# Keys and values pooled by VectorE in one reducing step each, and a free engine for the rests of the first weights

## The chip, the cores and the metric

The kernel runs on one core of a Trainium2 chip. The metric is the device time of one execution in microseconds (us), as the median of several runs. TensorE is written PE (PEld for its weight loads), VectorE DVE, ScalarE ACT, GpSimd POOL, and SyncE, which only issues transfers here, SP.

## The reference, cut to what matters

Eight batches of attention with pooled keys and values, then two wide feed-forward layers over 4608 tokens of 512 features. The part that the change touches is the pooling: eight neighbouring positions of a sequence of 576 are averaged into one, which leaves 72.

```python
# q, k, v: (8 batches, 8 heads, 576, 64) fp32
k_p = k.reshape(B, H, 72, 8, D).mean(axis=3)
v_p = v.reshape(B, H, 72, 8, D).mean(axis=3)
scores = scale * q @ k_p.transpose(0, 1, 3, 2)
attn_out = softmax(scores) @ v_p
# layer 1, x (8, 576, 512) from attn_out: u = x + (x^T U V)^T ; y = u + relu(u @ w_ch1) @ w_ch2
# layer 2: layer norm of y, then relu(yn @ w2_ch1) @ w2_ch2, added to y
```

## The kernel before

Every piece of work is declared as an operation with a price for each engine that may do it, with what it reads and writes, and with a priority. A planner in the file (`Order.schedule`) then lays all operations out in one go: it keeps a clock for each engine, gives an operation that two engines may do to the one that its prices favour, allocates buffers from rings, and treats VectorE and GpSimd as shut out of one another while both work on SBUF. The order that it arrives at is written into the program of each engine, and each engine follows its own list strictly. A changed price or a changed list of engines can therefore move any later operation.

The work goes through two heads at a time, called a pair: 32 pairs (`P`), four to a batch. For each pair SP loads `k` (128 rows: two heads by 64 features; 576 positions along a row), `q` and `v` (72 rows: one for each pooled position; for each head 8 times 64 numbers along the row). There is one buffer each for `k` and `v`, and two for `q`. `att_prep` pools the keys into `kp` and scales them into `kbd`; `att_prep_v` pools the values into `vs` (or `v1` for the first two batches, P below `TM` = 8); then come scores, softmax and the product with `vs`. From P = 8 on, `vs` holds a high part, rounded to the fp32r format, and the rest, so that two fast matmuls stand for one exact one; `split` makes such a pair of tensors.

In parallel the weights of layer 1 arrive as 64-bit floats. `load_w` decodes eight blocks of them in two halves each (lines 594 to 621, mostly VectorE), and splits each half into `wh` and its rest `wl` (line 556). The other weights are decoded later and parked in DRAM (`ahead`). The first eight blocks are used by `a_l1` (line 1291) and `a_l2` (line 1319) on tokens that are already through attention, while attention goes on for the later batches; this stretch ends near 600 us. After it three passes with the remaining weights run to the end (lines 1520 and 1608), with no pooling in them.

Before, the pooling of keys can be done by VectorE in one `tensor_reduce` (line 796) or by GpSimd in three halving additions (lines 799 and 800). The values are pooled by three halving additions, 512, 256 and 128 wide over both heads, each on either engine (line 827). The rest `wl` is for GpSimd alone.

Of the kernel before, what the change touches and what calls it, by code (L numbers as in the profile page):

```python
# [14 lines left out]
ALU = mybir.AluOpType  # L15
AX = mybir.AxisListType
# [3 lines left out]
B, H, S, D = 8, 8, 576, 64  # L20
DM = 512
NT = B * S
POOL = 8
SP = S // POOL
# [26 lines left out]
class Ring:  # L51


    def __init__(self, pool, shape, dtype, n, name, fifo=True):
        self.pool, self.shape, self.dtype, self.n, self.name, self.fifo = pool, shape, dtype, n, name, fifo
        self.tiles, self.free, self.made, self.turn = None, [(0.0, i) for i in range(n)], 0, 0
        pool.rings.append(self)
# [34 lines left out]
PE, ACT, DVE, GP, SY = "pe", "act", "dve", "pool", "sync"  # L92
# [273 lines left out]
def c_dve(n):  # L366
    return 68 + 1.042 * n


def c_fast(n):  # L370
    return 68 + 0.521 * n


def c_act(n, ps=False):
    return (51 if ps else 93) + 0.8333 * n


def c_pool(n):
    return 147 + 2.11 * n
# [28 lines left out]
def scaled(nc, e, dst, src, by):  # L408
    if e is nc.scalar:
        e.mul(dst, src, by)  # L410
    else:
        e.tensor_scalar(dst, src, by, None, op0=ALU.mult)
# [9 lines left out]
class Kern:  # L422
    def __init__(self, nc, tc, aps):
        self.nc, self.tc = nc, tc
        (self.qT, self.kT, self.v, self.U, self.V, self.wA, self.g, self.wC, self.out) = aps
        self.w_raw = [self.wA, self.wC]
        self.o = Order(nc, tc)
        att = Pool("att")
        stg = Pool("stg")
        slots = Pool("slots", side="right")  # L430
        w = Pool("wres", side="right")
        b1 = Pool("b1", after=[att])
        b2 = Pool("b2", side="right", after=[w])
        ps = Pool("ps", space=PSUM)
        self.pools = [stg, att, slots, w, ps, b1, b2]
        R = self.R = {}

        def ring(pool, name, shape, dt=F32, n=1, fifo=True):
            R[name] = Ring(pool, shape, dt, n, name, fifo)

        ring(stg, "wraw", [128, 512], I64)
        ring(stg, "wx", [128, 512])
        ring(stg, "wt", [128, 512])
        ring(att, "araw", [128, 512], I64)
        ring(att, "ax", [128, 512])
        ring(att, "at", [128, 512])
        ring(att, "kbd", [128, 2, SP], n=2)
        ring(att, "q", [128, S], n=2)
        ring(att, "k", [128, S])
        ring(att, "v", [SP, 2, POOL * D])  # L450
        ring(att, "kp", [128, SP], n=2)
        ring(att, "vs", [SP, 4, D], F32R, 3)
        ring(att, "vz", [SP, 3 * D], n=2)
        ring(att, "ef", [SP, 2, S])
        ring(att, "sc", [128, 5, 2 * SP], n=2)
        ring(att, "mx", [128, 10], n=2)
        ring(att, "sm", [128, 10], n=2)
        ring(att, "eh", [SP, 2, S], F32R)
        ring(att, "el", [SP, 2, S], F32R)
        ring(att, "avt", [128, SH], n=2)  # L460
        ring(att, "xT", [128, S], n=5)
        ring(att, "xh", [128, DM], F32R, 2)
        ring(att, "xl", [128, DM], F32R, 2)
        ring(att, "gr", [128, DM], F32R)
        ring(att, "gs", [128, DM], F32R)
        ring(att, "ust", [128, 5, 128], F32R)
        ring(att, "us", [128, 5, 128])
        ring(att, "vd", [128, S // 4], F32R, 2)
        ring(att, "v1", [SP, 2, D + 1], n=2)
        ring(att, "x4", [128, DM])  # L470
        ring(att, "ut", [128, 4 * 64])
        ring(att, "vstk", [128, S], F32R)
        ring(slots, "op", [128, SLOT], F32R, 16)
        ring(slots, "hid", [128, SLOT], F32R, 8)
        for f in range(NA):
            for a in "hl":
                ring(w, f"w{a}{f}", [128, 1024], F32R)
        ring(w, "xg", [128, NCC, TG])
        ring(w, "ys", [128, TG], n=2)
        for j in range(NSL):  # L480
            pool = b1 if j < NSL - 1 else b2
            for a in "hl":
                ring(pool, f"w1{a}{j}", [128, 7, 256], F32R)
                ring(pool, f"w2{a}{j}", [128, 2, 512], F32R)
        ring(b1, "xraw", [128, NCC, TG])
        ring(b1, "t3", [128, 2, TH])
        ring(b1, "t2", [128, 2, TH])
        ring(b2, "s12", [128, TG], n=2)
        ring(b2, "s5", [128, TH], n=2)
        ring(b2, "res", [128, NCC, TG], n=2)  # L490
        ring(b2, "yt", [128, NCC, TG])
        for a in ("lnh", "lnl"):
            ring(b2, a, [128, TG], F32R)
        for a in ("lns", "lnq"):
            ring(b2, a, [128, TG])
        for a in ("lnv", "lnd"):
            ring(b2, a, [128, TG // 128])
        ring(ps, "pa", [128, 512], n=2)
        ring(ps, "pbc", [128, 512], n=2, fifo=False)
        ring(ps, "py", [128, 512], n=4)  # L500
# [244 lines left out]
    def load_w(self, f, z, way):  # L745

        if z == 0:
            self.wres[f] = self.buf(f"wh{f}"), self.buf(f"wl{f}")
        wh, wl = self.wres[f]
        x = self.decoded(0, f, z, way)  # L750
        c = slice(z * 512, z * 512 + 512)
        self.split(View(wh, z, lambda t: t[:, c]), View(wl, z, lambda t: t[:, c]), View(x, None, lambda t: t), 512, hi_on=(ACT,), lo_on=(GP,))

    def ahead(self, layer, f, z):

# [32 lines left out]
    def att_prep(self, P):  # L788
        nc, o = self.nc, self.o
        q, k, v = self.raw[P]  # L790
        kp, kbd = self.buf("kp"), self.buf("kbd")
        kv = lambda: k.t.rearrange("p (n s) -> p n s", s=POOL)

        def pool(e):
            if e is nc.vector:
                e.tensor_reduce(kp.t, kv(), axis=AX.X, op=ALU.add)
                return
            for n in (4, 2):
                e.tensor_add(kv()[:, :, :n], kv()[:, :, :n], kv()[:, :, n : 2 * n])
            e.tensor_add(kp.t, kv()[:, :, 0], kv()[:, :, 1])  # L800

        o.op({DVE: c_dve(S), GP: c_pool(4 * SP) + c_pool(2 * SP) + c_pool(SP)}, pool, w=[k, kp])
        for h in range(2):
            r = slice(64 * h, 64 * h + 64)
            o.op(
                {ACT: c_act(SP), DVE: c_fast(SP)},
                lambda e, r=r, h=h: scaled(nc, e, kbd.t[r, h], kp.t[r], -1.0 / (POOL * 8)),
                r=[kp],
                w=[(kbd, h)],
            )  # L810
        self.qk[P] = (q, kbd)

    def att_prep_v(self, P):
        o = self.o
        v = self.raw[P][2]
        vs = self.vs[P] = self.buf("v1" if P < TM else "vz" if P < LEAN_T else "vs")
        n = POOL * D
        while n > D:
            n //= 2
            to, w = (lambda n=n: v.t[:, :, :n]), [v]  # L820
            if P < LEAN_T and n == D:
                to, w = (lambda: vs.t.rearrange("p (a d) -> p a d", d=D)[:, 0:3:2]), [v, vs]
                if P < TM:
                    to = lambda: vs.t[:, :, :D]
            o.op(
                {GP: c_pool(2 * n), DVE: c_dve(2 * n)},
                lambda e, n=n, to=to: e.tensor_add(to(), v.t[:, :, :n], v.t[:, :, n : 2 * n]),
                w=w,
            )
        if P < LEAN_T:  # L830
            return
        self.split(
            View(vs, 0, lambda t: t[:, 0:4:3]),
            View(vs, 1, lambda t: t[:, 1:3]),
            View(v, None, lambda t: t[:, :, :D]),
            2 * D,
        )

# [993 lines left out]
TM = 2 * NP  # L1832
E_BIAS = -40000.0
LEAN_T = 8
# [52 lines left out]
```

## Time and profile before

| | us |
|---|---|
| runs, median of 3 | 1762.2 (1757.46 to 1763.09) |
| the profiled execution, its own time | 1756.11 |
| its span in the trace | 1754.3 |
| PE busy in it | 1729.4 |
| DVE busy | 959.6 |
| POOL busy | 753.9 |

The span runs from the first to the last instruction. Busy time of PE counts a matmul from its start to its modelled end, so neighbouring matmuls overlap in it. A row that groups instructions gives the busy time of all of them, the mean of one in ns, and after the bar the idle time of the engine just before them, with what ended it.

### The profile page before, as it was taken

To read this page: it belongs to the slowest core of one execution; us is meant where nothing else is said; L and a number is where in the kernel's file an instruction comes from. 1 tells how busy PE (TensorE), PEld (TensorE's weight loads), DVE (VectorE), ACT (ScalarE), POOL (GpSimd) and SP (SyncE) were. 2 spreads that over 40 slices of the span, in tenths; PEclk is the share of its full clock that TensorE was granted. 3 is DMA by queue.
4 is the path that set the end of the run, shared out by engine and by line. 5 is a ranking of instruction groups with operands and counts; after the bars stand their busy time and mean duration, and the time that the engine had idled before them with its cause. 6 is when DMAs were issued, how large, how long until landed. Compare 5 with 4: busy or idle time off the path is not lost.

```text
span 1754.3 us, 27128 instructions
## 1 busy us (share of the span) xinstructions
PE 1729.4 (99%) x10302; PEld 1525.7 (87%) x10302; DVE 959.6 (55%) x1839; ACT 714.5 (41%) x1812; POOL 753.9 (43%) x655
## 2 busy tenths in 40 slices
PE   6999999999999999999999999999999999999998
PEld 6888888888888899999999889999999999999997
DVE  7998887888655344444445756553225633333333
ACT  5765655655522233333333443333333332223221
POOL 3442312311100166666667643333335455555554
PEclk9999999999999999999999999999999999999999
DMA  6665554555143334444443453431112422333322
GB/s 201 217 201 170 184 182 147 179 174 162 55 165 108 130 111 121 121 121 121 120 121 115 126 163 125 134 121 67 49 49 85 144 103 103 110 119 103 103 79 78
DMA packets 96691, 222.99 MB, mean 127 GB/s; under 512 B 15408, under 2 KB 15792, under 8 KB 90800
## 3 DMA queue, kind: packets, MB, share of 16 engines
q1 hardware_dynamic: 96416, 221.26, 39.9%
q8 instruction: 80, 1.31, 0.3%
q14 instruction: 51, 0.42, 0.1%
q10 hardware_dynamic: 144, 0.00, 0.0%
HBM read 151.85 MB, written 69.37 MB: 126 GB/s over the span
## 4 chain that ended last, share of the span: by engine, by line
PE 91%; DVE 2%; DMA 1%; POOL 0%; issue 0%; ACT 0%; DVEq 0%; POOLq 0%; ACTq 0%
PE py L1608 33%; PE pa L1520 17%; PE pbc L1520 13%; PE pbc L1319 11%; PE pa L1291 11%; PE py L398 2%; PE py L847 2%; PE py L978 1%; PE py L979 1%; PE py L1016 0%; PE py L1015 0%; DVE w1l L556 0%; PE py L1185 0%; PE pbc L1743 0%; DMA wraw<-w_d 0%
## 5 line engine op out<-in xcount | busy, mean ns | idle before, releaser
L1608 PE MATMUL py<-hid,w2h 128*128 128x512 f32 x1728 | 541.2, 394 | 0.2 <-DVE hid L1548 0.2
L1608 PE MATMUL py<-hid,w2l 128*128 128x512 f32 x864 | 338.7, 392 | 0.0
L1520 PE MATMUL pa<-op,w1h 128*128 128x256 f32 x1728 | 326.2, 281 | 1.4 <-DVE s L405 1.0
L1520 PEld LDWEIGHTS pa<-op,w1h 128*128 128x128 f32 x1728 | 293.8, 188 | 37.9 <-DVE s L405 1.5
L556 POOL TENSOR_TENSOR op<-xraw,op 128x512 fp32r<-128x512 f32 x130 | 171.9, 1324 | 276.9 <-ACT op L403 272.0
L1578 DVE TENSOR_TENSOR pbc<-s,pbc 128x512 f32<-128x512 f32 x108 | 75.2, 696 | 382.2 <-PE pbc L1520 382.2
L1608 PEld LDWEIGHTS py<-hid,w2h 128*128 128x128 f32 x1728 | 273.7, 189 | 11.1 <-DVE hid L1548 0.5
L1520 PEld LDWEIGHTS pbc<-op,w1h 128*128 128x128 f32 x1296 | 220.8, 188 | 28.1
L1520 PE MATMUL pbc<-op,w1h 128*128 128x256 f32 x1296 | 244.3, 281 | 0.0
L1520 PE MATMUL pa<-op,w1l 128*128 128x256 f32 x864 | 242.7, 281 | 0.0
L1608 PEld LDWEIGHTS py<-hid,w2l 128*128 128x128 f32 x864 | 162.5, 188 | 36.7
L1319 PE MATMUL pbc<-op,wh 128*128 128x512 f32 x576 | 182.1, 397 | 0.0
L1520 PE MATMUL pbc<-op,w1l 128*128 128x256 f32 x648 | 181.8, 281 | 0.0
L1291 PE MATMUL pa<-hid,wh 128*128 128x512 f32 x576 | 180.5, 394 | 0.0
L1520 PEld LDWEIGHTS pa<-op,w1l 128*128 128x128 f32 x864 | 163.0, 189 | 0.0
L1548 DVE SCALAR_TENSOR_TENSOR hid<-pa,hid 128x512 fp32r<-128x512 f32 x108 | 74.5, 690 | 125.1 <-ACT hid L1542 124.8
L1542 ACT ACTIVATE hid<-pa 128x512 fp32r<-128x512 f32 x108 | 64.6, 598 | 190.8 <-PE pa L1520 180.9
L1542 ACT ACTIVATE hid<-pbc 128x512 fp32r<-128x512 f32 x108 | 64.6, 598 | 180.4 <-DVE pbc L1578 179.5
L1474 POOL TENSOR_TENSOR t<-xraw 128x512 f32<-128x512 f32 x52 | 67.4, 1296 | 141.3 <-DMA xraw<-n_d 89.4
L1291 PEld LDWEIGHTS pa<-hid,wh 128*128 128x128 f32 x576 | 105.8, 188 | 21.3 <-DVE op L1298 0.2
L1520 PEld LDWEIGHTS pbc<-op,w1l 128*128 128x128 f32 x648 | 121.9, 188 | 0.0
L1319 PEld LDWEIGHTS pbc<-op,wh 128*128 128x128 f32 x576 | 103.8, 188 | 19.4
(210 smaller groups left out, 2864.2 us busy)
## 6 DMA issues: line engine op xcount, KB each, us to landing
xraw<-n_d SPq DMA_DIRECT2D x18, 1024.0 KB
wraw<-wC SPq DMA_DIRECT2D x32, 512.0 KB
wraw<-wA SPq DMA_DIRECT2D x24, 512.0 KB
w_d<-wx SPq DMA_DIRECT2D x48, 256.0 KB
wraw<-w_d SPq DMA_DIRECT2D x48, 256.0 KB
k<-kT SPq DMA_DIRECT2D x32, 288.0 KB
q<-qT SPq DMA_DIRECT2D x32, 288.0 KB
v<-v SPq DMA_DIRECT2D x32, 288.0 KB
```

The source lines that it names most:

```text
L398: e.matmul(out, src, ident, start=first, stop=True, is_transpose=True, skip_group_check=True)
L556: lambda e: e.tensor_sub(lo(), src(), hi().bitcast(F32)),
L847: lambda e: e.matmul(ps.t[:, i : i + 2 * SP], q.t[:, QT[t] : QT[t] + 128], kbd.t.rearrange("p h n -> p (h n)"), start=True, stop=True, ski ...
L978: e.matmul(ps.t[:, :SH], w, eh.t[:, h, c], start=True, stop=False)
L1291: e.matmul(ps.t, w.t[:, c], u.t, start=(i == 0), stop=(i == 3 * NCC - 1))
L1319: e.matmul(ps.t, w.t[:, c], x.t, start=(f == 0 and j == 0), stop=(f == NA - 1 and j == 2))
L1474: o.op(on, lambda e: e.tensor_sub(dst(), a(), c()), r=r, w=w)
L1520: e.matmul(bank.t[:, sl], w.t[:, self.WCOL[k], c], u.t[:, t], start=(first and i == 0), stop=(last and i == 5), skip_group_check=True,)
L1542: lambda e: e.activation(h.t[:, :TG], bank.t, AF.Relu),
L1548: lambda e: e.scalar_tensor_tensor(l.t[:, :TG], bank.t, 0.0, h.t[:, :TG].bitcast(F32), op0=ALU.max, op1=ALU.subtract),
L1578: o.op({DVE: c_dve(TG)}, lambda e: e.tensor_add(c.t, s.t, c.t), r=[s], w=[c])
L1608: e.matmul(y.t, w.t[:, i, c], x.t[:, :TG], start=(first and q == 0), stop=(last and q == 2))
```

## The change

Keys: only VectorE may pool them, in the one `tensor_reduce` that it had already. Values: only VectorE, in one `tensor_reduce` that reads `v` through the view `"p h (s d) -> p h d s"`, so that the eight numbers that are summed lie 64 numbers apart along the row; it reads 1024 numbers a row and writes 128. For P below `TM` it writes into `v1`; from then on into a new small buffer `vp` (one, 72 rows by 2 by 64), from which the split makes `vs`. Rests of the first weights: VectorE or GpSimd.

```diff
+        ring(att, "vp", [SP, 2, D])
...
-        self.split(View(wh, z, ...), View(wl, z, ...), View(x, None, ...), 512, hi_on=(ACT,), lo_on=(GP,))
+        self.split(View(wh, z, ...), View(wl, z, ...), View(x, None, ...), 512, hi_on=(ACT,))
...
-        def pool(e):
-            if e is nc.vector:
-                e.tensor_reduce(kp.t, kv(), axis=AX.X, op=ALU.add)
-                return
-            for n in (4, 2):
-                e.tensor_add(kv()[:, :, :n], kv()[:, :, :n], kv()[:, :, n : 2 * n])
-            e.tensor_add(kp.t, kv()[:, :, 0], kv()[:, :, 1])
-
-        o.op({DVE: c_dve(S), GP: c_pool(4 * SP) + c_pool(2 * SP) + c_pool(SP)}, pool, w=[k, kp])
+        o.op({DVE: c_dve(S)}, lambda e: e.tensor_reduce(kp.t, kv(), axis=AX.X, op=ALU.add), w=[k, kp])
...
-        while n > D:
-            n //= 2
-            to, w = (lambda n=n: v.t[:, :, :n]), [v]
...
-            o.op(
-                {GP: c_pool(2 * n), DVE: c_dve(2 * n)},
-                lambda e, n=n, to=to: e.tensor_add(to(), v.t[:, :, :n], v.t[:, :, n : 2 * n]),
-                w=w,
-            )
-        if P < LEAN_T:
+        vp = vs if P < TM else self.buf("vp")
+        to = (lambda: vp.t[:, :, :D]) if P < TM else (lambda: vp.t)
+
+        def pool(e):
+            e.tensor_reduce(to(), v.t.rearrange("p h (s d) -> p h d s", s=POOL), axis=AX.X, op=ALU.add)
+
+        o.op({DVE: c_dve(2 * n)}, pool, w=[v, vp])
+        if P < TM:
             return
...
-            View(v, None, lambda t: t[:, :, :D]),
+            View(vp, None, lambda t: t),
```

Not shown in it: `TM` and `LEAN_T` are both 8, and where `split` is given no engines for the rest, these are VectorE and GpSimd.

## Rows read from the trace of the kernel before

**Rows 1.** The page's head: span, and busy time of PE.
```profile
span 1754.3 us, 27128 instructions
...
PE 1729.4 (99%) x10302; PEld 1525.7 (87%) x10302; DVE 959.6 (55%) x1839; ACT 714.5 (41%) x1812; POOL 753.9 (43%) x655
```

**Rows 2.** Stretches: busy PE, PEld, DVE, ACT, POOL (instructions), PE clock, DMA.
```profile
0.00:20.00 20.00, 10.85 (x46) 9.83 (x47) 12.72 (x39) 9.95 (x31) 5.32 (x24) 1.00 0.74 215
20.00:60.00 40.00, 33.30 (x248) 29.38 (x247) 34.40 (x85) 26.21 (x81) 17.61 (x20) 1.00 0.67 206
60.00:96.00 36.00, 34.02 (x224) 29.56 (x223) 34.87 (x80) 21.57 (x67) 16.72 (x15) 1.00 0.63 199
96.00:200.00 104.00, 103.80 (x554) 86.86 (x553) 91.66 (x193) 66.05 (x233) 29.91 (x33) 1.00 0.62 196
96.00:500.00 404.00, 403.80 (x2140) 340.39 (x2139) 326.22 (x692) 232.20 (x812) 98.79 (x117) 1.00 0.51 161
600.00:1754.30 1154.30, 1147.47 (x7206) 1033.49 (x7204) 506.31 (x867) 398.92 (x778) 611.10 (x476) 1.00 0.35 111
```

**Rows 3.** Waits of PE in the first 96 us: total, times, longest.
```profile
PE py L847 <- DMA q<-qT: 5.3, 1, 5.3
PE py L847 <- issue: 3.8, 1, 3.8
```

**Rows 4.** Order of time, DVE and PE, 6.7 to 13 us: start, duration.
```profile
6.73 0.69 DVE L827 TENSOR_TENSOR v<-v 72x512 f32<-72x512 f32 x1 [1.84 <-DMA v<-v]
...
11.40 0.39 DVE L412 TENSOR_SCALAR kbd<-kp 64x72 f32<-64x72 f32 x2
...
11.89 1.30 PE L847 MATMUL py<-kbd,q 128*128 128x144 f32 x4 [3.80 <-issue]
```

**Rows 5.** One group of instructions on DVE, first 96 us.
```profile
L827 DVE TENSOR_TENSOR v<-v 72x512 f32<-72x512 f32 (+2 forms) x24 | 16.8, 702 | 2.5 <-DMA v<-v 2.4
```

**Rows 6.** Groups on POOL, first 96 us.
```profile
L799 POOL TENSOR_TENSOR k<-k 128x288 f32<-128x288 f32 (+1 forms) x12 | 10.0, 835 | 10.4 <-DMA k<-kT 10.0
L556 POOL TENSOR_TENSOR wl<-wx,wh 128x512 fp32r<-128x512 f32 x6 | 9.4, 1573 | 14.4 <-ACT wh L403 14.4
L556 POOL TENSOR_TENSOR wl<-ax,wh 128x512 fp32r<-128x512 f32 x6 | 8.2, 1367 | 18.8 <-ACT wh L403 18.8
L827 POOL TENSOR_TENSOR v<-v 72x256 f32<-72x256 f32 (+2 forms) x9 | 6.0, 664 | 11.0 <-DVE kp L796 4.9 <-DVE v L827 4.5 <-DVE sm L1050 1.2
L800 POOL TENSOR_TENSOR kp<-k 128x72 f32<-128x72 f32 x6 | 3.6, 604 | 0.5
```

**Rows 7.** DVE in the first 96 us again, shapes kept apart.
```profile
L613 DVE SCALAR_TENSOR_TENSOR ax<-araw,at 128x512 int32<-128x512 int32 x6 | 5.5, 921 | 0.4
L872 DVE TENSOR_REDUCE mx<-py 128x6 f32<-128x432 f32 x9 | 5.4, 597 | 2.2 <-PE py L847 2.2
L621 DVE SCALAR_TENSOR_TENSOR ax<-araw,ax 128x512 uint32<-128x512 uint32 x6 | 5.2, 869 | 0.1
...
L613 DVE SCALAR_TENSOR_TENSOR wx<-wraw,wt 128x512 int32<-128x512 int32 x6 | 5.1, 848 | 0.2
...
L872 DVE TENSOR_REDUCE mx<-py 128x4 f32<-128x288 f32 x9 | 4.0, 450 | 1.5 <-PE py L847 1.5
```

**Rows 8.** Lines 613, 796, 800 over the span: min/median/max ns.
```profile
L613 DVE SCALAR_TENSOR_TENSOR wx<-wraw,wt x57: 321/692/1821, 9.7 to 1184.5; 128x512 int32<-128x512 int32 x56, 128x160 int32<-128x160 int32 x1
...
L796 DVE TENSOR_REDUCE kp<-k x15: 722/746/753, 3.6 to 381.7; 128x72 f32<-128x576 f32 x15
...
L800 POOL TENSOR_TENSOR kp<-k x17: 312/329/992, 17.2 to 396.3; 128x72 f32<-128x72 f32 x17
```

**Rows 9.** A rest taken on VectorE: by shape, first 620 us.
```profile
L556 DVE TENSOR_TENSOR hid<-xg,hid 128x512 fp32r<-128x512 f32 x22 | 15.6, 718 | 0.8 <-ACT hid L403 0.6
```

**Rows 10.** One group on DVE from 96 to 500 us.
```profile
L827 DVE TENSOR_TENSOR v<-v 72x512 f32<-72x512 f32 (+2 forms) x22 | 14.6, 663 | 0.0
```

**Rows 11.** Waits of the SP queue in the first 96 us.
```profile
SPq L778 <- POOL kp L800: 11.1, 4, 4.2
```

More of the change, by code (lines that the diff above doesn't have):

```diff
@@ L751, in load_w @@
         c = slice(z * 512, z * 512 + 512)
-        self.split(View(wh, z, lambda t: t[:, c]), View(wl, z, lambda t: t[:, c]), View(x, None, lambda t: t), 512, hi_on=(ACT,), lo_on=(GP,))
+        self.split(View(wh, z, lambda t: t[:, c]), View(wl, z, lambda t: t[:, c]), View(x, None, lambda t: t), 512, hi_on=(ACT,))
     def ahead(self, layer, f, z):
@@ L817, in att_prep_v @@
         n = POOL * D
-        while n > D:
-            n //= 2
-            to, w = (lambda n=n: v.t[:, :, :n]), [v]
[L821 to L824, printed above, removed]
-            o.op(
-                {GP: c_pool(2 * n), DVE: c_dve(2 * n)},
-                lambda e, n=n, to=to: e.tensor_add(to(), v.t[:, :, :n], v.t[:, :, n : 2 * n]),
-                w=w,
-            )
-        if P < LEAN_T:
+        vp = vs if P < TM else self.buf("vp")
[4 more added lines that the diff above has]
+        if P < TM:
             return
```

## Prediction

> **What bounds the kernel now.** I read the page's head first. PE is busy 1729.4 of 1754.3 us [rows 1], so all that a change elsewhere can win or lose lies in PE's 25 us of idle time, or in new idle time. The busy times by stretch then say where those 25 us are [rows 2]: in the first 20 us PE idles 9.2, from 20 to 60 us 6.7, from 60 to 96 us 2.0, from 96 to 500 us only 0.2 in 404, and from 600 us to the end 6.8, where nothing is pooled. So two stretches matter. The first 96 us, where PE loses 17.8 us: there the eight pairs of the first two batches and the decoding of the first weights go through DVE, which is busy 69.3 of the 76 us from 20 to 96 (34.9 of the last 36); it is the bound there. And 96 to 500 us, where PE is full and DVE, at 326.2 of 404 us, works beside it. Third, PE's waits in the first 96 us [rows 3]: 5.3 us are the first load, which no pooling touches; the next, 3.8, ends at 11.9 us, just when DVE has scaled the second pair's pooled keys [rows 4].
>
> So the question is: how much work does DVE get, net, in the first 96 us, and does the cover hold after that?
>
> **The change part by part**, first 96 us.
>
> *Keys.* Six pairs were pooled on POOL (six last steps at line 800, twelve before them), 10.0 + 3.6 = 13.6 us of POOL, 2.3 us a pair [rows 6]. Each is now one reduction at 746 ns [rows 8]: DVE +6 × 0.746 = **+4.5 us**.
>
> *Values.* 24 additions on DVE took 16.8 us [rows 5] and 9 on POOL 6.0 us [rows 6]; 33 additions, three a pair, are 11 pairs. In their place stand 11 reductions over 1024 numbers, of a form that the trace doesn't show. The nearest rows: the key reduction reads 576 packed numbers in 0.746 us [rows 8], and the two maxima of line 872 differ by 147 ns for 144 numbers [rows 7], 1.02 ns a number. So 0.746 + 448 × 1.02 ns = 1.20 us if the wide step of the view costs nothing. The lower end is 1024 × 1.02 = 1.05 us. For the upper end I take the slowest rate of the rows for such data, POOL's 1367 ns for 512 [rows 6], 2.67 ns a number: 2.7 us. I take 1.20, the rate of the engine that does it: 11 × 1.20 − 16.8 = **−3.6 us** for DVE. Part of that gain is that the additions on DVE were often stretched while POOL worked.
>
> *Less stretching of other work.* Three groups of the decoding have means of 921, 869 and 848 ns here [rows 7], where the median of the same instruction is 692 [rows 8]; 6 × (229 + 177 + 156) ns = 3.4 us. The key reductions, in contrast, stay between 722 and 753 [rows 8]. POOL's work in the stretch is 13.6 + 6.0 for the pooling and 17.6 for the weights' rests [rows 6]; with the first two gone I take their share, 53%: **−1.8 us**. Bounds: 0 and −3.4.
>
> *Rests of the weights.* Twelve fall here, 1573 and 1367 ns each on POOL [rows 6]. A rest of the same shape costs DVE 718 ns [rows 9]. Which engine gets one is the planner's choice; POOL has little else to do now, and DVE is full, so I take three: **+2.1 us**; bounds 0 and 12 × 0.718 = +8.6. Where POOL keeps one, nothing changes.
>
> Sum for DVE: 4.5 − 3.6 − 1.8 + 2.1 = **+1.2 us**, on an engine that is the bound for most of the stretch.
>
> *Latency and the queues.* A pair's keys are ready in 0.74 us in place of 2.3, and the one `k` buffer comes free as much earlier. SP stands 11.1 us in four waits at the next load of `k` until POOL's last step is done [rows 11]; behind it in SP's list stand the loads of `q`, `v` and raw weights. Most pairs are prepared ahead, so I count this shortening once, 2.3 − 0.7 = **−1.6 us**. At the start, the first values' reduction holds DVE longer than the first addition did; the maxima and the decoding queued behind it move back by some 0.5 us (1.20 in place of 0.69 [rows 4]), and with them PE's wait of 3.8 us: **+0.5**. The new buffer `vp` adds a wait: the next values' reduction stands on DVE until the split before it has read `vp`. A split is long done when the next pair's values come; cost 0, and with the cover gone about one rest, 0.7 us.
>
> Together **about 0**: 1.2 − 1.6 + 0.5 = +0.1 us.
>
> *96 to 500 us.* Remaining: 11 key poolings, 11 × 0.746 = 8.2 us more; 21 pairs' values, 21 × 1.20 − 14.6 = +10.6 us [rows 10]. DVE goes from 326.2 to 345 of 404 us (85%); in its fullest part, 96 to 200 us, from 91.7 by a proportional 4.8 to 96.5 of 104. PE's own work hides that, as it hid 88% there [rows 2]; where the cover is gone, PE waits for DVE microsecond for microsecond. I count 0.
>
> [...] The value reduction steps 256 bytes from number to number, and no DVE row here reads so. POOL's last key addition steps 32 bytes and takes 329 ns in the median for 72 numbers [rows 8], 4.6 ns a number with all fixed costs in it; POOL's rests, with packed reads, take 2.67 [rows 6], and fixed costs can explain the gap, so the rows don't decide it. [...]
>
> **The rivals.**
>
> *The wide step halves DVE's reading rate: slower.* At 2 × 1.02 ns a number the reduction takes 0.746 − 0.588 + 2.09 = 2.25 us (the key row less its 576 numbers, plus 1024 at the doubled rate). Above 16.8 / 11 = 1.53 us the values cost DVE more than before; the time is longer by 5.3 us, which a measurement can tell, from about 1.20 + (5.2 + 3.4) / 11 = 1.98 us on, if half of DVE's 6.7 us of idle time between 20 and 96 us takes up the first 3.4. At 2.25 DVE gets 11 × 1.05 = 11.6 us more in the first 96 us, and 8 of them reach PE. From 96 to 500 us DVE gets 21 × 1.05 = 22 us more, 367 of 404, and 102 of 104 from 96 to 200: some 3 us more of waits, an estimate. In all +11: 1773. For it: no row reads in such steps, so none excludes it. [...] Against: decoding reads every second number at the rate of packed ones (692 ns for 512 [rows 8], 718 for packed [rows 9]).
>
> *The queue and the port open up: faster.* If each of SP's four waits for the key pooling shortens by 1.6 us and each shortening reaches PE through the loads behind it, PE gains 4 × 1.6 = 6.4 us of its 12.5 us of idle time past the first load: 1756. For it: PE's waits are for DVE's results, and DVE is stretched by POOL. Against: attention loads are ahead of use, and DVE's total doesn't fall.
>
> *The planner gives DVE most rests: slower.* Nine more of them at 0.718 us are +6.5 us in the bound stretch: 1768. Against: DVE is late in the plan and POOL empty.
>
> *Nothing moves:* the order is laid out anew and its small gains and losses cancel; this is in the forecast.
>
> **How the numbers follow.** The profiled execution took 1756.1 us, 6.1 below the median of the three runs (1762.2). The sum, +0.1, gives 1756.2 on its scale and 1762.3 on that of the median; since that median sits at the upper end of its runs, I state 1761.5. A measurement of this kernel can tell about 0.3%, 5.3 us, from no change. Chances: forecast 0.48, halved rate 0.26, rests on DVE 0.06, opened queue 0.20. So faster 0.20, same 0.48, slower 0.32. The likeliest case alone reaches from 1757 to 1767. The range takes in most of the halved rate above and the opened queue below: 1754.5 to 1774.
>
> **What would show it right or wrong.** The value reduction should read near 1.2 us in the trace; near 2.2 is the first rival. POOL should hold only rests in the first 96 us, mostly of weights, and DVE's busy time there should stay within 3 us of 82.0 (the first three stretches of [rows 2]). The decoding's means should fall towards 692 ns. PE's idle time should stay near 18 us in the first 96 us and near 0 up to 500 us. The prediction is wrong if PE shows waits for DVE between 96 and 300 us, or if the first matmuls of line 1291 come more than 4 us later or earlier than before.

## The result, and the profile after

The changed kernel takes 1772.71 us in the median of 11 runs (1768.43 to 1779.4) against 1763.09 for the kernel before (median of 11, measured beside it). The ratio is 1.0056, with a 95% interval of 1.0037 to 1.0076: slower by 0.56%, some 10 us. Two of the eleven runs of the kernel before, at 1891.19 and 5840.2 us, were far slower than the rest and are left out of the ratio; the median of the other nine is 1762.9. The forecast was no change, at 1761.5; its first rival, the wide step at 1773, is where the time fell.

The price in dispute comes first: line 815, the value reduction, over the whole span of the changed kernel (min/median/max in ns). The key reduction, line 795, stands beside it.

```profile
L795 DVE TENSOR_REDUCE kp<-k x32: 723/742/754, 3.6 to 406.9; 128x72 f32<-128x576 f32 x32
...
L815 DVE TENSOR_REDUCE vp<-v x24: 1926/1978/2003, 74.7 to 425.9; 72x128 f32<-72x1024 f32 x24
...
L815 DVE TENSOR_REDUCE v<-v x8: 1883/1898/1974, 6.7 to 68.0; 72x128 f32<-72x1024 f32 x8
```

Not 1.20 us, as the sum had it, and not the doubled rate of 2.25: 1.90 us for the first eight pairs and 1.98 for the other 24. The key reduction costs what it did [rows 8].

The stretches of the changed kernel, with the same columns as [rows 2]:

```profile
0.00:20.00 20.00, 10.00 (x53) 9.16 (x54) 13.96 (x35) 9.53 (x31) 2.30 (x19) 0.98 0.75 221
20.00:60.00 40.00, 35.49 (x236) 32.30 (x235) 35.76 (x80) 23.48 (x74) 6.58 (x5) 0.84 0.61 179
60.00:96.00 36.00, 34.73 (x206) 30.64 (x206) 34.84 (x70) 21.33 (x70) 4.55 (x3) 0.91 0.62 196
96.00:200.00 104.00, 97.81 (x518) 80.72 (x518) 92.67 (x181) 60.76 (x205) 16.74 (x14) 1.00 0.55 175
...
96.00:500.00 404.00, 395.64 (x2088) 329.07 (x2088) 346.29 (x696) 236.74 (x816) 42.42 (x35) 1.00 0.49 157
600.00:1772.80 1172.80, 1164.64 (x7280) 1047.81 (x7278) 510.24 (x875) 404.48 (x787) 611.17 (x476) 1.00 0.35 110
```

The reader is to see two things beside [rows 2]. From 96 to 500 us PE now idles 404 − 395.64 = 8.4 us, where it idled 0.2, and 104 − 97.81 = 6.2 of them lie before 200 us: the cover has gaps, though DVE is busy only 346.3 of 404 us (86%). Of this idle time 8.0 us are waits for DVE; the three largest are (96 to 500 us: total in us, times, longest):

```profile
PE py L835 <- DVE xT L974: 3.9, 4, 2.1
PE pbc L1307 <- DVE ys L405: 1.3, 1, 1.3
PE py L1004 <- DVE xl L557: 1.2, 1, 1.2
```

And PE's granted clock is 0.84 and 0.91 of full speed between 20 and 96 us, where the profiled execution of before had 1.00; the first experiment and the last section come back to that.

That DVE's work has come onto the path shows in the shares of the chain that ended last, from 200 to 460 us: first the changed kernel (the view itself ends the row there), then the kernel before, where the chain is PE's alone.

```profile
by line: PE pbc L1307 27.5%; PE pa L1279 19.2%; DVE vp L815 6.7%; PE py L398 6.4%; PE py L835 4.5%; DVE xT L974 4.2%; issue 3.6%; DVE el L557 3.5%; PE py L1004 2.1%; PE py L966 2.1%; PE py L967 2.1%; DVE op L1286 1.9%; DVE mx L860 1.8%; PE 
```

```profile
by line: PE pbc L1319 35.8%; PE pa L1291 34.5%; PE py L398 10.2%; PE py L847 7.6%; PE py L978 3.4%; PE py L979 3.3%; PE py L1016 1.8%; PE py L1015 1.8%; PE py L1185 1.6%
```

Within one batch the chain runs like this (start, duration, what), with the value reduction in it three times in 25 us:

```profile
401.41 1.98 DVE vp L815
...
413.54 1.96 DVE vp L815
...
426.01 1.91 DVE vp L815
...
428.77 0.68 DVE xl L557
429.50 0.50 PE py L1004
```

In between stand DVE's other work for attention and the decoding, and then PE goes on with what waited. PE idles only 2.2 us from 200 to 500, so this chain shows what PE's short waits hang on, not long idle time. Two marks on the way, for PE: first matmul of the first weights, and first matmul of the passes that follow (first and last start, in us, of the line).

```profile
L1279 PE MATMUL pa<-hid,wh x576: 387/389/802, 69.6 to 591.6; 128*128 128x512 f32 x192
...
L1508 PE MATMUL pa<-op,w1h x1728: 274/280/392, 613.8 to 1761.0; 128*128 128x256 f32 x192
```

In the profiled execution of before these stand at 61.8 and 598.3 us. So 7.8 us of the difference in span, 18.5 us, are there before 70 us, another 7.7 before 614, and 3 in the passes. The medians are only 10 us apart: that execution of before stood 6 us under its median and had a clock of 1.00 in the early stretches, so part of the 18.5 belongs to these two executions and not to the change.

### The profile page after: what moved, and what is told of

It is laid out like the page before. It is cut to its first block, busy times and chain, and to the rows that moved or that the text cites. A ratio compares the mean times of both kernels' runs of the same rounds, so it can differ in the third digit from the quotient of the medians.

```text
span 1772.8 us, 27002 instructions
## 1 busy us (share of the span) xinstructions
PE 1740.5 (98%) x10302; PEld 1531.9 (86%) x10302; DVE 990.6 (56%) x1845; ACT 720.5 (41%) x1821; POOL 671.4 (38%) x542
## 4 chain that ended last, share of the span: by engine, by line
PE 84%; DVE 7%; DMA 1%; ACT 1%; issue 1%; DVEq 0%; ACTq 0%; SPq 0%
PE py L1596 33%; PE pa L1508 17%; PE pbc L1508 13%; PE pbc L1307 9%; PE pa L1279 7%; PE py L398 1%; DVE vp L815 1%; PE py L835 1%; DVE xT L974 1%; DVE el L557 1%; DMA wraw<-wA 1%; DMA wraw<-w_d 1%; PE py L1004 0%; PE py L966 0%; DVE op L1286 0%
```

## The experiments

Theories. A: the wide step of the value reduction, some 0.75 us × 32 = 24 us more of DVE, costs the time. B: whatever else moved to VectorE and the new order cost it. C: the lower granted clock is a loss of its own. D: the planner's price for the reduction, 1135 ns, is too low, and an order laid out for the true one would not lose. Ratios are to the kernel before, measured beside each, with 95% intervals; they are worked out from the single runs and needn't be the quotient of two medians.

**The read alone.** Kernel e1 keeps every engine's list of instructions as the changed kernel has it, in the same order. Only the layout of v in memory differs, and with it the view. (The packing is done on the host, ahead of the device's time.)

```diff
-            e.tensor_reduce(to(), v.t.rearrange("p h (s d) -> p h d s", s=POOL), axis=AX.X, op=ALU.add)
+            e.tensor_reduce(to(), v.t.rearrange("p h (d s) -> p h d s", s=POOL), axis=AX.X, op=ALU.add)
...
-        "v": np.ascontiguousarray(v),
+        "v": np.ascontiguousarray(v.reshape(B, H, SP, POOL, D).transpose(0, 1, 2, 4, 3)).reshape(B, H, S, D),
```

> The changed kernel with one thing different: v is stored so that the eight numbers of a sum lie side by side, and the value reduction reads packed; every engine's list of instructions is the same. Theory A (the wide step of the reduction costs the time): the reduction falls from 1.9 to 1.98 us to about 1.20 us, DVE loses 32 x 0.75 = 24 us of work, and the time comes back to within 4 us of the kernel before, 1759 to 1767. Theory B (VectorE's extra operations and the new order cost it, whatever the step): the time stays at 1770 or more. Theory C (the fall of TensorE's granted clock between 15 and 70 us is a cause of its own, from the thinner new order): the clock stays down there and 4 us or more of the loss stay.

Measured: 1761.3 us, 0.9982 (0.9971 to 0.9993). The reduction, and the stretches (columns as in [rows 2]):

```profile
L815 DVE TENSOR_REDUCE vp<-v x24: 1202/1206/1218, 70.9 to 411.9; 72x128 f32<-72x1024 f32 x24
...
L815 DVE TENSOR_REDUCE v<-v x8: 1203/1212/1218, 6.0 to 64.2; 72x128 f32<-72x1024 f32 x8
```

```profile
20.00:60.00 40.00, 34.44 (x243) 30.40 (x243) 35.99 (x87) 26.52 (x85) 6.58 (x5) 0.91 0.72 205
60.00:96.00 36.00, 36.00 (x214) 32.09 (x214) 32.52 (x72) 20.41 (x64) 5.83 (x4) 0.91 0.59 181
...
96.00:500.00 404.00, 402.20 (x2131) 337.88 (x2131) 333.68 (x702) 237.49 (x819) 39.55 (x34) 1.00 0.52 161
```

With packed reads the reduction takes 1.21 us, PE idles 1.8 us from 96 to 500 us, and the loss is gone. The chain that ended last, from 200 to 460 us, is PE's alone again:

```profile
by line: PE pbc L1307 36.2%; PE pa L1279 34.1%; PE py L398 10.3%; PE py L835 7.7%; PE py L966 3.3%; PE py L967 3.3%; PE py L1004 1.8%; PE py L1003 1.8%; PE py L1173 1.6%
```

1.0056 / 0.9982 = 1.0074 is the price of the wide step in one and the same order: 13 us, uncertain by some 4. Theory A holds, and B falls for the change as a whole. C falls as a loss of its own: the clock is 0.91 here between 20 and 96 us, and the kernel is faster than the one before all the same. A second measurement, as the gain over before is small:

> The all packed form a second time, beside the one before, since its gain of 0.18% is small: 1758 to 1764, ratio 0.996 to 1.000 to the kernel before.

1761.54 us, 0.9990 (0.9977 to 1.0004). The gain over the kernel before is thus at the edge of what can be told; the step's price is not.

**One part at a time**, each in the kernel before. Keys only:

```diff
-        o.op({DVE: c_dve(S), GP: c_pool(4 * SP) + c_pool(2 * SP) + c_pool(SP)}, pool, w=[k, kp])
+        o.op({DVE: c_dve(S)}, lambda e: e.tensor_reduce(kp.t, kv(), axis=AX.X, op=ALU.add), w=[k, kp])
```

> The kernel before with the first part alone: keys on VectorE only. Theory A: no wide step in it, within 3 us of before (1760 to 1766). Theory B: a third to a half of the loss, +3 to +5 us, as 17 x 0.746 = 12.7 us move to VectorE.

1768.72 us, 1.0026 (1.0010 to 1.0042): some 4.5 us, what theory B expects of this part and more than the 3 that A allows. Values only, with `att_prep_v` and the buffer `vp` of the changed kernel:

```diff
+        ring(att, "vp", [SP, 2, D])
...
+        o.op({DVE: c_dve(2 * n)}, pool, w=[v, vp])
```

> The kernel before with the second part alone: values on VectorE in one reduction with the wide step. Theory A: most of the loss, +7 to +12 us (1770 to 1775). Theory B: about half of it, +4 to +6 us.

1776.98 us (5 runs), 1.0065 (1.0052 to 1.0078): the whole loss, as theory A has it (the median lies 2 us above A's range). Rests only:

```diff
-        self.split(..., 512, hi_on=(ACT,), lo_on=(GP,))
+        self.split(..., 512, hi_on=(ACT,))
```

> The kernel before with the third part alone: rests of the first weights on either engine. Theories A and B: within 3 us of before; a rival, that rests given to VectorE hold up the first stretch, expects +3 us or more.

1765.68 us, 1.0014 (0.9993 to 1.0035): nothing that can be told. The three parts add up to 1.0105, the change has 1.0056: each kernel has an order of its own, and the parts can't be added.

**The other way to pool on VectorE.** The changed kernel with the three additions of before, VectorE only:

```diff
-        o.op({DVE: c_dve(2 * n)}, pool, w=[v, vp])
+        for m in (4 * D, 2 * D, D):
+            dst = to if m == D else (lambda m=m: v.t[:, :, :m])
+            o.op(
+                {DVE: c_dve(2 * m)},
+                lambda e, m=m, dst=dst: e.tensor_add(dst(), v.t[:, :, :m], v.t[:, :, m : 2 * m]),
+                w=[v, vp] if m == D else [v],
+            )
```

> The changed kernel with the values pooled on VectorE by the three halving additions of before, keys on VectorE and rests on either engine. Theory A: no wide step, three additions take 0.68 + 0.41 + 0.28 = 1.37 us a pair in place of 1.9 to 1.98, so 1760 to 1768. Theory B (whatever moves to VectorE costs): 1770 or more.

1759.88 us, 0.9977 (0.9964 to 0.9989): faster than before. The additions take 21.7 + 17.1 + 9.6 + 2.3 = 50.7 us of DVE, the changed kernel's reductions 47.3 + 15.3 = 62.6 (busy time of these lines up to 620 us). Everything that the change moves to VectorE is there, 32 key and 32 value poolings, and it gains; with the one wide step in place of the three additions the kernel loses. This is theory A against B a second time, though in an order of its own and with runs at a slightly higher mean clock (0.996 to 1.0, beside 0.991 to 1.0), and the fastest kernel here that needs no other layout in memory.

**Packed values, all else as before:**

```diff
+        o.op({DVE: c_dve(2 * n)}, pool, w=[v, vp])   # view "p h (d s) -> p h d s", v stored packed; keys and rests as before
```

> The kernel before with one thing changed: v is stored packed and pooled on VectorE in one reduction; keys and rests as before. Theory A: as fast as the all packed form or better, 1757 to 1763. Theory B: slower than before by 2 us or more, since all 32 poolings stand on VectorE.

1765.01 us, 1.0001 (0.9989 to 1.0013): the forecast of neither; no loss and no gain.

**An honest price.**

```diff
-        o.op({DVE: c_dve(2 * n)}, pool, w=[v, vp])
+        o.op({DVE: 1900}, pool, w=[v, vp])
```

> The changed kernel with the planner told 1900 ns for a value reduction in place of 1135, so that it lays the order out for what the reduction takes. Theory D (the reduction costs time because the order was laid out for a shorter one): most of the loss goes, 1762 to 1767. Theory A (VectorE's 24 us more work cost the time in any order): 1768 to 1775, within 4 us of the changed kernel.

1774.32 us, 1.0048 (1.0029 to 1.0066). The loss stays: theory D falls, as far as one order can show it.

**Where the step costs.** The changed kernel with v packed for the first eight pairs only, and for the other 24 only; lists of instructions the same again.

```diff
+            e.tensor_reduce(to(), v.t.rearrange("p h (d s) -> p h d s" if P < TM else "p h (s d) -> p h d s", s=POOL), ...)
```

> The changed kernel with v stored packed for the first two batches (8 pairs) alone; the lists of instructions are the same. If the wide step costs its time in the first 96 us, where VectorE is the bound, as the prediction's first rival has it (8 of 11 us), this takes back 8 us or more of the changed kernel's loss against the all packed form (13 us): 1762 to 1766. If it costs it later, 1769 to 1774.

1771.35 us, 1.0037 (1.0020 to 1.0053).

> The complement: packed for the later six batches (24 pairs) alone, same lists. By the prediction's first rival it takes back some 3 us: 1768 to 1772. If the later stretch, where VectorE stood at 86% and covered by TensorE, is where the time goes, it takes back 8 us or more: 1762 to 1766.

1764.51 us, 0.9998 (0.9985 to 1.0012). Both times are those expected for a cost in the later stretch (1769 to 1774 and 1762 to 1766). Packing the first pairs takes back 0.2%, which is not clear of noise, packing the later ones 0.6%. From 96 to 500 us, first e7 and then e8:

```profile
96.00:500.00 404.00, 396.84 (x2088) 329.81 (x2087) 344.35 (x692) 235.67 (x814) 40.96 (x34) 1.00 0.50 156
```

```profile
96.00:500.00 404.00, 401.61 (x2132) 337.35 (x2131) 333.86 (x700) 236.69 (x817) 39.50 (x34) 1.00 0.51 160
```

With the later pairs packed PE idles 2.4 us there, with the first ones packed 7.2. The two marks on PE's way, in e1, say the same:

```profile
L1279 PE MATMUL pa<-hid,wh x576: 387/389/802, 64.8 to 577.8; 128*128 128x512 f32 x192
```

```profile
L1508 PE MATMUL pa<-op,w1h x1728: 273/280/386, 600.0 to 1748.1; 128*128 128x256 f32 x192
```

Between e1 and the changed kernel, which share their lists, the first mark moves by 69.6 − 64.8 = 4.8 us and the second by 13.8: 9 us are lost after the first, 6.6 of them as PE's idle time from 96 to 500 us (8.4 less 1.8). In e7 the marks stand at 65.1 and 607.7, in e8 at 67.7 and 603.1. The time goes mostly where the prediction had seen cover. Of the 4.8 us before the first mark only 1.5 are more idle time; in the other 3.3 PE is busy longer with the same 329 matmuls, at a mean clock of 0.86 in place of 0.92. Whether the wide step brought that lower clock isn't shown.

**By way of the queue?** In the changed kernel SP stands 19.7 us in five waits for the value reduction before it may load `v` again (first 200 us), and raw weights stand behind it.

```profile
SPq L783 <- DVE vp L815: 19.7, 5, 7.0
```

```diff
-        ring(att, "v", [SP, 2, POOL * D])
+        ring(att, "v", [SP, 2, POOL * D], n=2)
```

> The changed kernel with two buffers for v in place of one, so that the next load of v need not wait for the long reduction, and the loads behind it in SP's list (raw weights among them) aren't held up by it. Theory A1 (the long reduction costs through VectorE's own time): the loss stays, 1769 to 1775. Theory A2 (it costs through the v buffer and SP's list, where the loads of v stood 20 us in five waits for it): half of the loss or more goes, 1762 to 1768.

1786.0 us (6 runs), 1.0114 (1.0097 to 1.0131): neither. The kernel got slower by another 0.6%. The second buffer gives the planner another order, and the wait is still there, 12.9 us in six, so this run doesn't decide between A1 and A2. In e1, whose waits there are 15.7 us in six and nearly the same, the loss was gone: these waits by themselves don't make it. But in the changed kernel the chain from 96 to 170 us passes through loads of raw weights, while in e1's, from 96 to 500 us, no load is among the thirteen largest shares, which go down to 0.5%. The changed kernel, 96 to 170 us:

```profile
by line: DMA wraw<-wA 13.3%; PE pbc L1307 8.1%; DVE vp L815 7.8%; DVE xT L974 5.9%; DVE el L557 5.7%; issue 5.5%; ACT sc L869 3.8%; DVE wx L622 3.4%; DVE op L1286 3.4%; PE py L398 3.3%; DVE mx L860 2.8%; DVE wx L614 2.6%; DVE wt L602 2.1%; 
```

So how much of the wide step's price reaches PE through DVE's own list, and how much through late loads of weights, stays open.

**The step by itself.** Kernel m1 leaves the computation out and only measures: the same 1024 numbers a row, summed by eights, with the step from number to number in the tile's name (in numbers of 4 bytes; `red64s` steps 256 bytes).

> A kernel that leaves the reference's computation out and only measures: VectorE reductions of the same 1024 numbers to 128 sums with 4, 8, 16, 32, 64, 256 and 512 bytes from number to number, four of each, then additions on VectorE, copies on ScalarE and additions on GpSimd at growing steps. [...] A rival, that only steps above some larger width cost: 1.2 us up to 32 or 64 bytes. A rival, that the cost grows with the step: 512 bytes slower than 256.

```profile
L33 DVE TENSOR_REDUCE red8s<-src 128x128 f32<-128x1024 f32 x4 | 7.9, 1975 | 0.0
L33 DVE TENSOR_REDUCE red4s<-src 128x128 f32<-128x1024 f32 x4 | 7.8, 1958 | 0.0
L33 DVE TENSOR_REDUCE red128s<-src 128x128 f32<-128x1024 f32 x4 | 7.5, 1865 | 0.0
L33 DVE TENSOR_REDUCE red64s<-src 128x128 f32<-128x1024 f32 x4 | 7.5, 1863 | 0.0
L33 DVE TENSOR_REDUCE red16s<-src 128x128 f32<-128x1024 f32 x4 | 7.4, 1850 | 0.0
L33 DVE TENSOR_REDUCE red1s<-src 128x128 f32<-128x1024 f32 x4 | 4.9, 1214 | 1.1 <-DMA src<-v 1.1
L33 DVE TENSOR_REDUCE red2s<-src 128x128 f32<-128x1024 f32 x4 | 4.8, 1211 | 0.0
...
L49 POOL TENSOR_TENSOR gps4s<-src 128x64 f32<-128x64 f32 x4 | 1.7, 432 | 0.0
...
L39 DVE TENSOR_TENSOR add4s<-src 128x128 f32<-128x128 f32 x4 | 1.5, 380 | 0.0
...
L49 POOL TENSOR_TENSOR gps2s<-src 128x64 f32<-128x64 f32 x4 | 1.4, 356 | 0.0
L49 POOL TENSOR_TENSOR gps1s<-src 128x64 f32<-128x64 f32 x4 | 1.3, 328 | 3.7 <-DMA src<-v 3.7
...
L39 DVE TENSOR_TENSOR add2s<-src 128x128 f32<-128x128 f32 x4 | 1.2, 288 | 0.0
L39 DVE TENSOR_TENSOR add1s<-src 128x128 f32<-128x128 f32 x4 | 1.2, 288 | 0.0
```

1.21 us at 4 and 8 bytes, 1.85 to 1.98 from 16 bytes on, and no more at 512 than at 64. It is a single stair between 8 and 16 bytes, worth (1863 − 1214) / 1024 = 0.63 ns a number at the change's 256 bytes (0.74 at 32, the dearest), not something that grows.

## Why the prediction was wrong, step by step

*The step that failed* is "I take 1.20, the rate of the engine that does it". The lower end, 1.05, and the upper, 2.7, held the true price, 1.90 to 1.98 us; the choice between them went by the nearest packed row, though no row read in such steps. The sum for DVE in the first 96 us, −3.6 us for the values, becomes 8 × 1.908 + 3 × 1.971 − 16.8 = +4.4, and the whole sum +9.2 in place of +1.2. The doubt about the 256-byte step, raised against the change, was the better lead; the test of it with POOL's 32-byte step could decide nothing, and e1's same lists with packed reads (1.21 us) show that the step was the whole matter.

*The first rival* was right in kind and in its total, 1773 forecast and 1772.7 measured. Its size was off: the rate was taken as halved (2.25 us), a factor of two that no run shows; it is lower by 1863 / 1214 = 1.53 in m1 and 1978 / 1206 = 1.64 in the kernel. And so was its place. It put 8 of 11 us into the first 96 us and 3 after them. The runs show the reverse: of the 0.74% between the packed and the wide form, packing the later 24 pairs (three of them pooled before 96 us) gives back 0.58% and the first eight 0.19% (1.0056 less 0.9998 and 1.0037), where each of these differences is uncertain by some 0.25%. That the total fits is therefore luck: with the mean price measured, 62.6 / 32 = 1.96 us, its own working gives 11 × 0.76 − 3.4 = 4.9 us before 96 us and at most 3 after, some 1770, and too high a price made up for too small a loss behind the cover.

*The cover from 96 to 500 us* failed with it. Forecast: DVE 345 of 404 us at 1.20, hidden, and 367 at 2.25, with some 3 us of waits. Measured: 333.7 with packed reads and 1.8 us of PE's idle time (e1), 346.3 with wide ones and 8.4. The share alone doesn't decide it: in e6, with another order, DVE is as busy and PE idles 1.5 us.

```profile
96.00:500.00 404.00, 402.49 (x2122) 337.70 (x2121) 345.09 (x759) 230.53 (x804) 33.46 (x31) 1.00 0.52 162
```

In the changed kernel the reductions, the splits and the sums of a batch follow one another on DVE, and the chain passes through them; what spares PE in e6 was not taken apart. "As it hid 88% there" was read from one order of work and doesn't carry to another. With that, two signs that the prediction had named for being wrong are there: PE waits for DVE between 96 and 300 us, 6.8 us in all, and the first matmul of the first weights comes 7.8 us later than in the profile of before (at a mean clock of 0.86 up to there, in place of 1.00; what part that has in it was not taken apart).

*The other parts* hold in their prices. Keys: one reduction at 742 ns, as priced; alone they cost 1.0026, in the order that goes with them. That cost was only measured, its cause not taken apart. Rests: three taken for VectorE in the first 96 us, and the planner gave it three (line 557, two of 682 ns and one of 676). Less stretching: two of the three decoding groups fell from 869 and 921 ns to 685 and 678, near the 692 expected; line 614 on `wx` rose to 1034. In sum DVE was busy 84.6 us in the first 96, within the 3 us of 82.0 that were allowed, but it got less done: on `ax` it ran five of each decoding step in place of six. PE had begun 495 matmuls in the first three stretches in place of 518. Its idle time there, 15.8 us, was even below the 18 forecast, but it was busy longer with fewer matmuls (80.2 us in place of 78.2), at a mean clock of 0.89 in place of 1.00.

*With 1.20 us the forecast would have held:* e1 is that kernel, and 1761.3 and 1761.5 us are what was forecast for the change (1761.5), 0.1 to 0.2% under the kernel before.

## What to carry to other kernels

Price a reduction through a rearranged view by the bytes between the numbers that it reads one after another: in m1's reductions of 1024 fp32 numbers they came at 1.2 ns apiece up to 8 bytes, all fixed costs included, and at 1.8 to 1.9 from 16 bytes on, whatever the step up to the 512 bytes measured. Where a layout can be chosen when the data is stored, let the summed numbers lie side by side; where it can't, halving additions over contiguous halves (three instructions in place of one) were the faster form here, 0.9977 against 1.0056. And a mean busy share below 90% is no proof of cover (85% on DVE cost PE 1.5 us in e6, 86% cost 8.4 in the changed kernel): look at whether the engine's pieces stand in one chain within a period.

## What the runs showed of the hardware that was not expected

The stair stands in other instructions too (rows of m1): VectorE's additions over 128 numbers take 288 ns at 4 and 8 bytes and 380 at 16, GpSimd's over 64 numbers 328, 356 and 432 at 4, 8 and 16.

The kernel before is not always at full clock. Its profiled execution shows a granted clock of 1.00 in every stretch of [rows 2], but in the 29 timed runs beside e1 to e4 the mean clock of an execution lay between 0.992 and 0.998, and the times between 1758.4 and 1769.5 us; the changed kernel's lay between 0.990 and 0.997. Over these 29 runs the time falls by some 0.5 us for each 0.001 of mean clock, with much scatter (correlation −0.33); from 0.995, their mean, to the 0.999 of the profiled execution that is some 2 us, an estimate, so the clock explains a part of the 6.1 us by which that execution stood under the median, and the rest is open. The lower clock of the changed kernel's profile (0.84 and 0.91 of full speed between 20 and 96 us, with 0.50 from 35 to 40 and from 65 to 70) is no mark of the change: between 20 and 60 us the clock is 0.72 in the profile of e9, which loses nothing, and 1.00 in that of e11, which loses most.

An order laid out anew can cost or save as much as the change itself: a second buffer, meant to take a wait away, made the kernel some 10 us slower, and three parts that cost 0.26, 0.65 and 0.14% alone cost 0.56% together.
